# A gated mix of a long convolution and a token MLP: transform tables loaded as constants, and all instructions in a fixed order

## The chip, the cores and the metric

The kernel runs on one core of a Trainium2 chip. The metric is device microseconds (us) of one execution, from the launch's first to last work on the device. The kernel before was run three times: 179.86, 182.16 and 179.96 us, median 179.96. Five engines work side by side and are kept in step by semaphores: TensorE (PE, matrix products), VectorE (DVE), ScalarE (ACT), GpSimd (POOL) and SyncE (SP), which here only issues DMAs.

## The reference

Two branches are mixed by a gate per row. S is 2048, D is 640 and F is 1536; everything is bf16.

```python
g = sigmoid((q * gate_w).sum(-1))
# branch A: short shift convolution of k, times v, then a long convolution
k_shift = sum(k_pad[:, t:t + S, :] * shift_k[:, 3 - t] for t in range(4))
kv = k_shift * v
y = irfft(rfft(kv, 2 * S) * rfft(ssm_k, 2 * S))[:S] + kv * ssm_D
a = q * y
# branch B: an MLP over the tokens
h = layernorm(q)
b = (gelu(h^T @ w1 + b1) @ w2 + b2)^T
out = g * a + (1 - g) * b
```

## The kernel before, in words

**Transforms.** The long convolution is done by a transform of length 4096 at odd frequencies, split into four residues p = 0..3 of the position, and two halves h of the sequence. Inside a residue the transform is a matrix product with tables of cosines and sines, 128 x 128 blocks held in `FTB` (L580, 1 MB over 128 partitions). `fwd` (L880) and `fwd_even` (L896) do it on PE: 320-column matmuls into one of four PSUM slots, evacuated by ACT. The filter `ssm` is transposed on PE first (`transp`, L862, "wtr"), evacuated to `wT`, and transformed ("W"); kv is transformed in two halves ("A"). Between the residues DVE adds and subtracts (`mixing`, `cross`, `product`, `invmix`). `inverse` (L1263) goes back by PE with the same tables in another layout.

**Tables.** They are made on the chip. POOL writes index rows (`brow`, `acol`, eight `jrow`, L806), DVE multiplies and adds them and masks to 12 bits (`prod`, `tb`, `pint`), ACT takes the sine (`sins`, L833). For the inverse, four DMA transposes copy `FTB` to `GTB` (L1044), and later four ACT copies (`gil`, L1114) write them back to `FTB` interleaved.

**MLP.** q is loaded as four blocks `X` of 512 rows. DVE takes the statistics (`bn_stats`, 32 halves, and 16 aggregates), POOL the power -1/2, DVE normalises in place. The first product ("m1") has 12 groups `ft` of 32 matmuls, each group in one PSUM slot, in four parts `hk` of eight; W1 comes in three chunks of four 512 KB pieces through two buffers `ring`. The second product ("m2") has 16 groups of 24 matmuls.

**Short convolution.** k is loaded (`k_load`), permuted by a DVE copy into `kp`, and turned by a DMA transpose to `KT` (`k_turn`, L760); PE multiplies it with banded tap matrices `KF` that POOL built ("kv", 16 short matmuls a group); ACT evacuates and DVE multiplies with v (L1054). `kn` shares the memory of the second ring, so W1's second chunk waits for it.

**Order.** Each engine runs its instructions in the order in which they are emitted. `_Sched.add` (L359) collects operations with their dependencies; `_Sched.run` (L389) simulates them with the estimated durations `dur`, priorities `prio` and PSUM slots while the program is built, and emits in the order found. `chain=True` on a DMA keeps it behind the DMA chained before it. DMAs from SP are issued in order: one that waits holds up those behind it. POOL issues DMAs that add into their target (`accum`). `SPIN` (L798) puts matmuls of zeros ("zz") ahead of the transposes. Lines that many groups share in the profile are those of helpers: L298 is every matmul, L676 every ACT instruction, L632 and L646 DVE or POOL arithmetic, L272 and L265 plain and transposing DMAs.

Of the kernel before, what the change touches and what calls it, by code (L numbers as in the profile page):

```python
# [9 lines left out]
BF16 = mybir.dt.bfloat16  # L10
# [303 lines left out]
class _Op:  # L314
    __slots__ = ("eng", "dur", "emit", "prio", "idx", "ndep", "succ", "vt", "vtrole", "end", "start", "kind", "lat", "deps", "name", "after", "nafter", "asucc", "lock")
# [13 lines left out]
class _Sched:  # L329
# [29 lines left out]
    def add(self, eng, dur, emit, reads, writes, prio=None, vt=None, lat=0.0, name=""):  # L359
# [9 lines left out]
        if vt is not None:  # L369
            vt.left += 1  # L370
            if vt.last_pe is not None:
                deps.add(vt.last_pe)
            if eng == "PE":
                if vt.first is None:
                    vt.first = op
                vt.last_pe = op
            else:
                for d in deps:
                    if d.vt is not vt and not vt.keep:
                        if d not in vt.first.deps:  # L380
                            vt.first.deps.add(d)
        op.deps = deps
        op.after = set()
        self._rec(op, reads, "R")
# [4 lines left out]
    def run(self):  # L389
        ops = self.ops  # L390
        for op in ops:
            op.succ = []
            op.asucc = []
            op.ndep = len(op.deps) + len(op.after)
        for op in ops:
            for d in op.deps:
                d.succ.append(op)
            for d in op.after:
                d.asucc.append(op)
        engs = list(ENGS) + ["SP", "QA"]  # L400
        ready = {e: [] for e in engs}
        pend = {e: [] for e in engs}
        free = {"ACT": 2.93, "DVE": 0.85, "POOL": 0.83, "PE": 1.18, "SP": 0.0, "QA": 0.0}
        port = {"DVE": 0.0, "POOL": 0.0}
        dma_free = 0.3
        avail = {}
        for op in ops:
            avail[op] = 0.0
            if op.ndep == 0:
                heapq.heappush(pend[op.eng], (0.0, op.prio, op.idx))  # L410
        nfree = list(range(self.NSLOT))
        held = {}
        events = []
        order = []
        t = 0.0
        done = 0
        started = 0
        n = len(ops)
        frees = []
        while started < n:  # L420
            while frees and frees[0][0] <= t:
                _, sl, cls = heapq.heappop(frees)
                nfree.append(sl)
                held[cls] -= 1
            nxt = []
            progress = False
            for e in engs:
                while pend[e] and pend[e][0][0] <= t:
                    _, p, i = heapq.heappop(pend[e])
                    heapq.heappush(ready[e], (p, i))  # L430
                if free[e] > t:
                    nxt.append(free[e])
                    continue
                skipped = []
                pick = None
                while ready[e]:
                    p, i = heapq.heappop(ready[e])
                    op = ops[i]
                    if op.vt is not None and op.vt.slot is None:
                        c = op.vt.cls  # L440
                        if not nfree or held.get(c, 0) >= self.limit.get(c, 99):
                            skipped.append((p, i))
                            continue
                    pick = op
                    break
                for s in skipped:
                    heapq.heappush(ready[e], s)
                if pick is None:
                    if pend[e]:
                        nxt.append(pend[e][0][0])  # L450
                    continue
                op = pick
                progress = True
                started += 1
                if op.vt is not None and op.vt.slot is None:
                    op.vt.slot = nfree.pop(0)
                    held[op.vt.cls] = held.get(op.vt.cls, 0) + 1
                op.start = t
                if e in ("SP", "QA") or op.lat < 0:
                    issue = 1.2 if e == "POOL" else 0.1  # L460
                    s = max(t + issue, dma_free)
                    dma_free = s + op.dur
                    op.end = dma_free + 2.0 + (6.0 if e == "POOL" else 0.0)
                    free[e] = t + issue
                else:
                    op.end = t + op.dur
                    if op.lock:
                        op.end += max(port["POOL" if e == "DVE" else "DVE"] - t, 0.0)
                        port[e] = op.end
                    free[e] = op.end  # L470
                order.append(op)
                if op.vt is not None:
                    op.vt.left -= 1
                    if op.vt.left == 0:
                        heapq.heappush(frees, (op.end + 0.05, op.vt.slot, op.vt.cls))
                for s in op.asucc:
                    avail[s] = max(avail[s], op.start)
                    s.ndep -= 1
                    if s.ndep == 0:
                        heapq.heappush(pend[s.eng], (avail[s], s.prio, s.idx))  # L480
                for s in op.succ:
                    lat = 0.08 if s.eng == e else 0.15
                    if e == "PE" and s.eng == "PE":
                        lat = 0.0
                    avail[s] = max(avail[s], op.end + lat)
                    s.ndep -= 1
                    if s.ndep == 0:
                        heapq.heappush(pend[s.eng], (avail[s], s.prio, s.idx))
                nxt.append(free[e])
            if not progress:  # L490
                c = [x for x in nxt if x > t]
                if frees:
                    c.append(frees[0][0])
                assert c, "schedule stuck: " + str([(o.name, o.eng, o.ndep) for o in ops if not hasattr(o, "end")][:12])
                t = min(c)
        self.order = order
        self.makespan = max(o.end for o in ops)
        return order
# [6 lines left out]
def bass_gated_mix__ssm_conv_h3__mixer_token_mlp__prompt_kernel(  # L505
    nc, A_q, A_k, A_v, A_shift_k, A_ssm_k, A_ssm_D, B_x, B_w1, B_b1, B_w2, B_b2, gate_w, out
):
    with nc.Block() as blk:

        @blk.tensor  # L510
        def _(pe_engine):
            _build(nc, A_q, A_k, A_v, A_shift_k, A_ssm_k, A_ssm_D, B_x, B_w1, B_b1, B_w2, B_b2, gate_w, out)


def _build(nc, A_q, A_k, A_v, A_shift_k, A_ssm_k, A_ssm_D, B_x, B_w1, B_b1, B_w2, B_b2, gate_w, out):
# [10 lines left out]
    with ExitStack() as es:  # L526
# [54 lines left out]
        GTB = alloc("GTB", [128, 4, 2, 2, 2, 128], BF16)  # L581
# [6 lines left out]
        acol = alloc("acol", [128, 1], I32, at=base_of(SS))  # L588
        brow = alloc("brow", [128, 128], I32, at=base_of(SS) + 64)
        prod = alloc("prod", [128, 128], I32, at=base_of(SS) + 64 + 2048)  # L590
        tb = alloc("tb", [128, 2, 2, 128], I16, at=base_of(SS) + 64 + 2560)
# [13 lines left out]
        pint = alloc("pint", [128, 4, 2, 2, 256], I16, at=base_of(ring[1]))  # L605
        jrow = alloc("jrow", [128, 8, 256], I16, at=base_of(ring[1]) + 8192)
# [7 lines left out]
        cgb = [alloc(f"cgb{i}", [128, 2, D], BF16, at=base_of(GTB) + 2560 * i) for i in range(3)]  # L614
# [7 lines left out]
        def dve_dur(n, mode):  # L622
            return n / {1: 960.0, 2: 1920.0, 4: 3840.0}[mode] + (0.04 if mode == 4 else 0.08)

        def act_dur(n, nap=0):
            return n / 1200.0 + 0.09 + 0.05 * nap
# [32 lines left out]
        def act(o, i, func, bias=None, scale=None, acc=None, vt=None, prio=None, name="act"):  # L659
# [17 lines left out]
            return SC.add("ACT", act_dur(n_of(o), nap), emit, rr if vt is not None else rr + [i], ww, prio=prio, vt=vt, name=name)  # L677
# [34 lines left out]
        last = [None]  # L712

        def dma(o, i, nbytes, stream="SP", prio=None, sem=None, rate=365.0, chain=False, **kw):
# [7 lines left out]
            if chain:  # L722
                if last[0] is not None:
                    o_.after.add(last[0])
                last[0] = o_
# [14 lines left out]
        def ssm_load(h, a, b):  # L740
            dma(ssm[:, a:b, 1024 * h:1024 * h + 1024], dr(A_ssm_k, 128 * S * a + 1024 * h, [[S, 128], [128 * S, b - a], [1, 1024]]), 128 * (b - a) * 2048, chain=True, rate=({0: 262.0, 1: 223.0}.get(a, RL3)) if h == 0 else 385.0)
# [9 lines left out]
        def x_load(hk):  # L751
            dma(X[:, hk, :, :], dr(A_q, 512 * hk * D, [[4 * D, 128], [1, 4 * D]]), 128 * 5120, chain=True, rate=(352.0 if hk == 0 else 415.0))
# [614 lines left out]
```

## Time and profile before

| what | value |
|---|---|
| median of the three runs | 179.96 us |
| the profiled execution: span from first to last instruction | 178.7 us (the profile gives no other time of it) |
| PE busy | 170.9 us, 1373 matmuls |
| DVE busy | 169.5 us, 203 instructions |
| ACT busy | 117.0 us |
| POOL busy | 43.1 us |
| DMA | 43.51 MB, mean 243 GB/s |
| granted TensorE clock, mean | 0.999 |

PE and DVE columns are the time in which the engine had an instruction in work; the ends of matmuls are modelled and neighbours overlap by some 0.16 us. A line of a timeline has start, length, engine, line of the kernel, operation, written and read names, shape, count, and in brackets the idle time before it with what ended it. A line of the chain of waits has start, length and what the chain ran through. A line of the DMA view has what was loaded, the queue, count, size and the median time from issue to landing.

### The profile page before, as it was taken

The page shows a single profiled execution, that of the slowest core. Times are in us where ns is not written, and L with a number is a line of the kernel's source. Part 1 is how long each engine was busy: PE and PEld are TensorE (multiplying, and loading weights), DVE is VectorE, ACT ScalarE, POOL GpSimd, SP SyncE. Part 2 cuts the span into 40 slices and gives each one's busy share as a digit, 9 for nine tenths or more (in the row PEclk, how much of TensorE's full clock was granted, in tenths as well). Part 3 has the DMA queues.
Part 4 walks back from the last instruction along what each step waited for, and adds up shares of the span by engine and source line. Part 5 has one row for each costly group of instructions (what it writes and reads, how often), then busy time and mean ns, then how long its engine had stood idle before and what let it go on. Part 6 is the DMA issues. An engine that isn't in the chain of part 4 may idle for free.

```text
span 178.7 us, 3326 instructions
## 1 busy us (share of the span) xinstructions
PE 170.9 (96%) x1373; PEld 128.4 (72%) x1374; DVE 169.5 (95%) x203; ACT 117.0 (65%) x176; POOL 43.1 (24%) x52
## 2 busy tenths in 40 slices
PE   7868999899999999999999999999999999999993
PEld 2545787487778677776777778888888887777772
DVE  7799889979999999999999899999999999999984
ACT  4998997999899999428999921131231323753760
POOL 8099803100000065000241100403525000252000
PEclk9999999999999999999999999999999999999999
DMA  5999999999999999999499989797999999599463
GB/s 145 384 413 372 388 301 206 264 421 299 213 258 289 189 272 235 229 229 231 97 244 285 173 132 363 158 229 241 171 194 221 208 201 394 205 164 236 114 233 138
DMA packets 38542, 43.51 MB, mean 243 GB/s; under 512 B 15867, under 2 KB 31360, under 8 KB 38528
## 3 DMA queue, kind: packets, MB, share of 16 engines
q1 hardware_dynamic: 33296, 32.16, 59.1%
q0 software_dynamic: 5200, 11.14, 35.8%
q8 instruction: 11, 0.18, 0.4%
q14 instruction: 3, 0.02, 0.0%
q10 hardware_dynamic: 32, 0.01, 0.0%
HBM read 25.87 MB, written 2.62 MB: 159 GB/s over the span
## 4 chain that ended last, share of the span: by engine, by line
PE 88%; DMA 6%; ACT 3%; SPq 2%; issue 0%; DVE 0%
PE pp L298 88%; DMA rows<-in_B_b_dram 6%; SPq L272 2%; ACT C L676 1%; ACT L676 1%; ACT GT L676 0%; DVE O L688 0%
## 5 line engine op out<-in xcount | busy, mean ns | idle before, releaser
L632 DVE TENSOR_TENSOR C<-C 128x2560 bf16<-128x2560 bf16 (+2 forms) x37 | 54.5, 1525 | 1.1 <-ACT C L676 1.1
L298 PE MATMUL pp<-X,ring 128*128 128x320 bf16 x384 | 55.4, 299 | 0.0
L298 PE MATMUL pp<-GT,W 128*128 128x320 bf16 x384 | 52.6, 299 | 0.0
L298 PEld LDWEIGHTS pp<-GT,W 128*128 128x128 bf16 x384 | 43.6, 114 | 8.6
L298 PEld LDWEIGHTS pp<-X,ring 128*128 128x128 bf16 x384 | 37.3, 98 | 14.3
L676 ACT ACTIVATE C<-pp 128x640 bf16<-128x640 f32 x64 | 40.5, 737 | 3.2 <-PE pp L298 3.2
L676 ACT ACTIVATE O<-pp,c,omg 128x640 bf16<-128x640 f32 x15 | 13.3, 884 | 34.7 <-PE pp L298 34.7
L267 POOL DMA_DIRECT2D C<-C x8 | 11.0, 1615 | 45.0 <-DVE C L632 45.0
L298 PE MATMUL pp<-wT,FTB 128*128 128x320 bf16 x112 | 17.1, 299 | 1.4 <-ACT wT L676 0.8
L676 ACT ACTIVATE cgb<-pp,gg 128x640 bf16<-128x640 f32 x16 | 12.7, 794 | 5.7 <-PE pp L298 5.3
L676 ACT ACTIVATE GT<-pp,cc 128x640 bf16<-128x640 f32 x12 | 9.6, 801 | 9.0 <-PE pp L298 9.0
L298 PEld LDWEIGHTS pp<-wT,FTB 128*128 128x128 bf16 x112 | 10.5, 98 | 6.5 <-ACT wT L676 1.2
L945 DVE BATCH_NORM_STATS2 stats<-X 128x6 f32<-128x320 bf16 x32 | 13.5, 461 | 1.1 <-DMA X<-in_A_q_dram 1.1
L632 DVE TENSOR_TENSOR tm<-C,C 128x2560 bf16<-128x2560 bf16 (+1 forms) x7 | 14.3, 2060 | 0.0
L298 PE MATMUL pp<-C,FTB 128*128 128x320 bf16 x96 | 13.4, 299 | 0.0
L267 POOL DMA_DIRECT2D C<-q_hi x6 | 5.9, 977 | 27.6 <-DVE C L632 13.1
L298 PEld LDWEIGHTS pp<-C,FTB 128*128 128x128 bf16 x96 | 9.3, 98 | 3.8 <-issue 0.2
L676 ACT ACTIVATE gq<-gq 128x640 bf16<-128x640 bf16 x16 | 11.8, 739 | 0.1
L632 DVE TENSOR_TENSOR SS<-C 128x2560 bf16<-128x2560 bf16 x8 | 11.7, 1488 | 0.1
L632 DVE TENSOR_TENSOR C<-tm 128x2560 bf16<-128x2560 bf16 (+1 forms) x9 | 10.7, 1194 | 0.1
L676 ACT ACTIVATE ksh<-pp 128x1024 bf16<-128x1024 f32 (+1 forms) x12 | 9.9, 903 | 0.2 <-PE pp L298 0.2
L676 ACT ACTIVATE wT<-pp 128x1024 bf16<-128x1024 f32 x10 | 9.7, 1027 | 0.6 <-PE pp L298 0.6
(77 smaller groups left out, 188.8 us busy)
## 6 DMA issues: line engine op xcount, KB each, us to landing
ring<-in_B_w_dram SPq DMA_DIRECT2D x12, 512.0 KB, 9.6
W<-in_B_w_dram SPq DMA_DIRECT2D x12, 512.0 KB, 6.3
C<-C POOLq DMA_DIRECT2D x8, 640.0 KB, 10.6
X<-in_A_q_dram SPq DMA_DIRECT2D x4, 640.0 KB, 9.0
kn<-in_A_k_dram SPq DMA_DIRECT2D x4, 640.0 KB, 9.3
out_dram<-O SPq DMA_DIRECT2D x7, 320.0 KB, 3.2
C<-SS POOLq DMA_DIRECT2D x3, 640.0 KB, 11.7
ssm<-in_A_ssm_k_dram SPq DMA_DIRECT2D x3, 512.0 KB, 7.4
```

The source lines that it names most:

```text
L267: ins = engobj.dma_start(out_ap, in_ap, accum_op=ALU.add, max_dma_last_dim=2560)
L272: ins = engobj.dma_start(out_ap, in_ap)
L298: ins = self.nc.tensor.matmul(ps_ap, lhsT=lhsT, rhs=rhs, start=start, stop=stop, skip_group_check=True)
L632: o_ = SC.add(eng, d, lambda s: T.op(eng, lambda e: e.tensor_tensor(o, a, b, op), rd, [o]), rd, [o], prio=prio, name="tt")
L676: return T.op("ACT", lambda e: e.activation(o, src, func, **kw), rr + [src], ww)
L945: ops.append(SC.add("DVE", 0.38, (lambda o, i: lambda s: T.op("DVE", lambda e: e.bn_stats(o, i), [i], [o]))(o, i), [i], [o]))
```

## The change

The tables are computed on the host while the program is built and stored with the program as two constants, `ftab` and `gtab`, 1 MB each. `FTB` is loaded in two DMAs on SP, residues 0 and 2 and then 1 and 3; `GTB`, with a layout of its own for the inverse, in one. All table arithmetic on POOL, DVE and ACT, the four table transposes and the four interleaving copies are removed. The bias rows are loaded from ACT's queue. All matmuls of zeros now stand in one block of 16 at the start. ACT's first instruction is a GELU of one column. Filter blocks 1 and 3 of the first half are evacuated by DVE. `SSM0` is two pieces. The statistics are taken in four groups of four.

The scheduler is removed. `follow` takes a written list of 647 operation numbers, in the sequence of their `add`, as the order, and a string of PSUM slots. Dependencies that only ordered the first matmul of a PSUM slot behind what the evacuation reads become `hint`, which orders nothing.

```diff
+    def follow(self, order, slots):
+        vts, done = {}, set()
+        for op in self.ops:
+            if op.vt is not None and id(op.vt) not in vts:
+                vts[id(op.vt)] = op.vt
+        for vt, s in zip(vts.values(), slots):
+            vt.slot = s
+        self.order = [self.ops[i] for i in order]
...
+def _tables():
+    def cs(k):
+        a = 2.0 * np.pi / 4096.0 * (np.asarray(k, np.int64) % 4096)
+        return np.stack([np.cos(a), np.sin(a)])
...
+                f[:, p, k2, kt] = np.moveaxis(cs(m * (8 * q + 4 * kt + p)), 0, 1)
+            g[:, p, :, k2] = np.moveaxis(cs((4 * (q - 128 * k2) + 1) * (4 * n + p)), 0, 1)
...
+        ftab, gtab = (nc.inline_tensor(a, name=n).ap() for a, n in zip(_tables(), ("ftab", "gtab")))
...
-        SSM0 = ((0, 1), (1, 3), (3, 5))
+        SSM0 = ((0, 2), (2, 5))
+        DVE_EV = (1,3)
+        def tab_load(i, w):
+            dma(V(FTB, 1024 * i, [[2048, 2], [1, w]]), dr(ftab, 2048 * i, [[4096, 128], [1024, 2], [1, w]]), 128 * 4 * w, tok=f"f{i}")
-        small(rows[0:4, 1, :], dr(B_b2, 0, [[512, 4], [1, 512]]), 4096, "SP", chain=True)
+        small(rows[0:4, 1, :], dr(B_b2, 0, [[512, 4], [1, 512]]), 4096, "QA")
...
-        SPIN = (7, 2, 1, 1, 1)
+        SPIN = (0, 0, 0, 0, 0)
+        mms(_VT("cv"), spin(16), name="spin").dur = 5.0
+        act(cst[:, 0:1], cst[:, 1:2], ACT.Gelu_apprx_tanh, name="table").dur = 1.6
-        for p in PORD:
-            t_ = tt("DVE", pv, V(tb, 0, [[0, 2], [256, 2], [1, 256]]), V(jrow, 512 * p, [[256, 2], [0, 2], [1, 256]]), ALU.add)
-            pprev = ts("DVE", pa, pa, 4095, None, ALU.bitwise_and, mode=4)
-            sins[p] = act(FTB[:, p, :, :, :, :].rearrange("q a b c d -> q (a b c d)"), pa, ACT.Sin, bias=cst[:, 0:1],
...
+            if h == 0 and db in DVE_EV:
+                evac_dve(o, i, vt, prio=0)
-            gtbs.append(dma(GTB[:, p, :, :, :, :].rearrange("q a b c d -> q (a b c) d"), FTB[:, p, :, :, :, :].rearrange("q a b c d -> q (a b c) d"), 128 * 2048, rate=200.0, transpose=True, chain=True))
+        dma(GTB[:, :, :, :, :].rearrange("q a b c d -> q (a b c d)"), dr(gtab, 0, [[4096, 128], [1, 4096]]), 128 * 8192, tok="g")
-                    gil = act(V(FTB, 1024 * p, [[1, 2], [256, 4], [2, 128]]), V(GTB, 1024 * p, [[512, 2], [128, 4], [1, 128]]), ACT.Copy, prio=10 ** 5, name="gil")
-        SC.run()
+        SC.follow([int(i) for i in _ORDER.split()], [int(i) for i in _SLOTS])
+_ORDER = """
+8 0 9 4 10 6 11 5 1 13 12 20 16 7 14 21 15 221 26 2 17 27 32 25 29 33 28 22 3 23 18 19 24 36 30 37 34 31 154 40 35 38
...
```

Counted out, the list gives SP this order: filter 512 and 768 KB, X 0, table residues 0 and 2, X 2, table residues 1 and 3, X 1, the filter's second half (768 and 512 KB), X 3, W1 pieces 0 and 1, k 1, W1 2, k 0, gate weights, W1 3, transposes of k 1 and k 0, k 2, k 3, v 0, transpose of k 2, v 1, W1 piece 1 of chunk 1, transpose of k 3, W1 0 of chunk 1, v 3, and then the rest of W1, v 2 and `gtab`.

## The prediction, before the changed kernel was run

> **What bounds the kernel now.** I read the page first, then the chain of work that ended last, then the timelines of TensorE (PE), VectorE (DVE), ScalarE (ACT) and SyncE's queue (SP), then the landings of the loads.
>
> ```profile
> span 178.7 us, 3326 instructions
> PE 170.9 (96%) x1373; PEld 128.4 (72%) x1374; DVE 169.5 (95%) x203; ACT 117.0 (65%) x176; POOL 43.1 (24%) x52
> ```
>
> PE and DVE are both full, so a gain needs both to end earlier. The chain of work says from when PE alone decides:
>
> ```profile
> 4.64 10.14 DMA rows<-in_B_b_dram
> ...
> 14.82 16.34 PE pp L298 x143
> ...
> 32.50 1.28 ACT L676
> ...
> 35.92 140.11 PE pp L298 x1128
> ```
>
> From 35.92 us PE runs 140.11 us without a gap. Whatever is won or lost before that moves the end; behind it only a new wait matters. PE's timeline shows the losses:
>
> ```profile
> 11.41 0.30 PE L298 MATMUL pp<-wT,FTB 128*128 128x320 bf16 x1
> 12.47 1.67 PE L298 MATMUL pp<-wT,FTB 128*128 128x320 bf16 x11 [0.77 <-ACT wT L676]
> 14.82 0.38 PE L298 MATMUL pp<-ident,rows 4*128 4x4 bf16 x5 [0.68 <-DMA rows<-in_B_b_dram]
> 15.13 7.24 PE L298 MATMUL pp<-wT,FTB 128*128 128x320 bf16 x52
> ...
> 34.64 1.04 PE L298 MATMUL pp<-wT,FTB 128*128 128x320 bf16 x4 [0.51 <-ACT GT L676]
> ```
>
> The first transform (wT,FTB) starts at 11.41. It waits for the evacuation of the transposed filter (ACT wT), not for a table. DVE's timeline, start and length in the first two columns, gives a price for dependent neighbours:
>
> ```profile
> 8.28 1.28 DVE L945 BATCH_NORM_STATS2 stats<-X 128x6 f32<-128x320 bf16 x3 [1.08 <-DMA X<-in_A_q_dram]
> ...
> 116.17 1.49 DVE L632 TENSOR_TENSOR C<-C,SS 128x2560 bf16<-128x2560 bf16 x1
> 117.70 1.49 DVE L632 TENSOR_TENSOR C<-tm 128x2560 bf16<-128x2560 bf16 x1
> ```
>
> The second overwrites what the first reads and starts 1.53 us later; independent ones run at 1.40 (two in 2.89).
>
> **The yardstick.** The page gives the execution's span, 178.7 us, and no other time of its own. The runs' median is 179.96, so 1.26 us lie around the span; I carry them over.
>
> PE between 11.41 and 35.92 (24.51 us): 136 matmuls of 320 columns (64 first transform, 56 MLP, 16 second transform) at 0.136 us (320 of them in 43.63) are 18.5; 40 transposes (24 in 1.65, 16 in 1.15) 2.5; constants 0.3. That is 21.3 of work and 3.2 of loss. So PE's end = start of the first transform + 21.3 + 140.1 + waits; before, 11.4 + 21.3 + 3.2 + 140.1 = 176.0.
>
> **The change, part by part.**
>
> *Table arithmetic out.* Gone are eight DVE operations on pint (4 x 0.68 + 4 x 0.43 = 4.4 us), three on prod and tb (0.9), ten POOL iotas, and four Sin (3.36 + 1.14 = 4.5 on ACT). None ends a wait of PE after 4.3 us; three Sin do delay the first evacuation to 7.02. The last filter piece ended PE's wait at 9.63 and two evacuations (2.04) followed. Alone their removal is worth nothing, covered by the filter's load; without that cover the 1.9 us from 5.15, when the first transposes ended, to 7.02.
>
> *Tables in by DMA, another order of loads.* Landings before, from issue plus time to landing, by megabytes queued: 0.79 at 6.3 us, 1.44 at 8.3, 1.97 at 9.6, 2.6 at 11.2, 3.9 at 14.1, 5.8 at 19.5: 2.5 to 2.8 us per MB. The order list, counted out, loads filter (1.31 MB), X block 0, half the table, X 2, the other half, X 1, second filter half, X 3, W1. Hence filter 7.8, X 0 9.6, first tables 10.8, second 13.7, W1's first piece 22.2 (before 19.5). The last transposes run 7.9 to 10.0; two of five evacuations move to DVE; the last on ACT ends at 11.1. First transform at 11.2: -0.2. No row shows a 1024-column evacuation on DVE. Nearest are ACT's, 0.92 each (five in 4.69), and the final DVE reads of PSUM, 0.55 for 320 columns, so 1.76 if scaled. I take 1.15, nearer to ACT's row; the upper end puts DVE 0.6 later, the lower 0.2 earlier. DVE sits idle there until X 0.
>
> *Spins.* Sixteen 512-column matmuls stand at the front. The first seven took 3.16, so 0.43 each; a later pair 0.59, so 0.215 each. Half and half they end at 6.4, all at 0.43 at 8.1; the filter's second piece at 7.8 covers the first and leaves 0.3 of the other.
>
> *The early constants and the table load.* Bias rows go to ACT's queue before X, so PE's stop from 14.1 to 15.13 (1.0) goes. One activation table at the start replaces the load at 32.50, and PE's 0.51 behind it goes. The row has the next ACTIVATE 1.30 us after that load began. [...]
>
> *What is late next at the start.* Thirteen evacuations at 0.60 (14 in 8.45) from 11.9 end at 19.7. Two wide (0.92) and two narrow ones then free the PSUM slot of the first MLP group: 22.8. Its W1 (22.2) and its normalised X (22.5, after X 3's first statistics at 21.1) come just before. PE's own work ends at 11.2 + 10.6 = 21.8: a wait of 1.0.
>
> *Table transposes and interleaving copies out.* Four DMA transposes held SP for 9.97 us (51.7 to 61.7) and four ACT copies took 5.1. W1's third chunk waits behind the former but is used from about 90; ACT sat idle 9.0 us for PE around the latter. Worth nothing under that cover (up to 10 us if the chunk were wanted at 62); one 1 MB load on SP replaces them, used after 150.
>
> *The fixed order.* SP is where it can bite:
>
> ```profile
> 24.03 7.36 SPq L265 DMA_TRANSPOSE KT<-kp  x2
> 31.43 1.06 SPq L272 DMA_DIRECT2D vkv<-in_A_v_dram  x2
> ```
>
> A transpose of k holds SP 3.7 us. Before, all four v loads went out ahead of the second pair; now v 1 is queued behind transpose 2, which waits for a DVE copy, which waits for k 2. From statistics at 9.8: 30 halves (0.383), 14 aggregates (0.09) and 10 applies (0.36) are 16.4, with 0.5 for X 3's landing: copy of k 1 at 26.7, of k 0 ending at 29.9. Transposes hold SP 27.4 to 34.8. k 2 lands 4.9 later, like the first load behind transposes before (vkv): 39.7. DVE reaches its copy at 38.4 and waits 1.3. Transpose 2 holds SP 40.5 to 44.2; v 1 is issued then. For its landing the loads' rows (median us last) give the ends:
>
> ```profile
> vkv<-in_A_v_dram SPq DMA_DIRECT2D x2, 640.0 KB, 5.4
> v<-in_A_v_dram SPq DMA_DIRECT2D x2, 640.0 KB, 9.5
> ```
>
> Singly 4.9 to 10.5. I take 4.9, as it too is the first plain load behind a transpose: 49.1. DVE wants it at 40.5 + 5 x 1.405 + 0.735 = 48.2, waits 0.9 and multiplies until 50.5. PE's order needs the product 26.5 us after the first MLP group (14 MLP groups of 1.087, 17 transform groups, 80 short matmuls in 4.2): 49.3. With PE's list fixed, nothing fills: a wait of 1.4. The other gates have covers of 0.3 to 3 us, for which I put 0.2: last normalised X 34.2 against 35.3, k transposed 37.8 against 40.7. On POOL the tap products (8.14) run from 7.6 and the scales follow from 15.8, wanted at 18.6. Late on POOL three accumulating DMAs move behind that of the third product, to 133 (first before 124.5); at 10.6 us they land by 146.4, wanted at 147.5.
>
> *DVE.* Busy 163.3 us between 8.28 and 176.6, idle 5.0. Now it starts at 9.8 and idles 3.5 (0.5, 1.3, 0.9, and 0.8 in small gaps). Of some twenty dependent neighbours about ten are pulled apart, 0.13 each, -1.3. End 9.8 + 163.3 - 1.3 + 3.5 = 175.3, 1.3 earlier, level with PE. [...]
>
> **Sum.** PE ends at 11.2 + 21.3 + 140.1 + 1.0 + 1.4 + 0.2 - 0.3 (constants now earlier) = 174.9, 1.1 before the old 176.0. The end behind it is unchanged. 179.96 - 1.1 = 178.8 us.
>
> **The rivals.**
>
> *v 1 comes late (slower).* At 10.5 us it lands at 54.7; PE waits 54.7 + 1.6 - 49.3 = 7.0 instead of 1.4: 184.4. It is slower than before from a landing time of about 6 us, slower by over 2% from 9.7. For it: DMA busy at 1.0 or more there. Against: little is queued ahead of it.
>
> *DVE is the bound.* If pulling pairs apart saves nothing, DVE ends at 176.6: 180.0. For it: 95% busy. Against: the 1.53.
>
> *The tables' megabyte delays all that follows.* 2.7 us on X, W1 and k instead of the 1.0 counted: 180.5. For it: DMA full until 45 us. Against: X 0 is early.
>
> *No wait at all (faster).* Start 0.5 earlier, no waits: 178.8 - 2.6 - 0.5 = 175.7. For it: every gate is within 2 us. Against: four would have to hold.
>
> *The change does nothing.* The tables were never waited for, and PE and DVE stay full: 180.0.
>
> **How the numbers follow.** Likeliest 0.45 (own range 177.2 to 180); DVE bound, late tables or no change 0.32 (179.5 to 181.5); v 1 late 0.14, most of it over 2%; no wait 0.09. 2%, about what a measurement of this kernel tells from no change, is 176.4 to 183.6. Faster 0.09, same 0.79, slower 0.12. The range runs from 176.0 to 183.6 and leaves out the ends of the last two cases.
>
> **What would show it.** First transform at 11.2; first MLP matmul at 22.8; no second table load; PE's only long gap near 49, ended by DVE's product, with DVE waiting for v 1 shortly before; last matmul near 175. It is wrong if the first transform starts after 12, if v 1 lands over 6 us after its issue, if dependent neighbours are as common as before on DVE, or if PE stops after 60 us.

## The result, and the profile after

The changed kernel took 186.53 us (median of four runs, 185.21 to 187.26), the kernel before 179.91 (four runs, 179.31 to 182.16) beside it: a ratio of 1.035, 95% interval 1.029 to 1.042. The prediction was 178.8 us, with a range that ended at 183.6. Ratios leave out single runs more than 1.5% above the fastest of their kernel; medians do not.

The profiled execution took 185.21 us with a span of 183.1, so 2.1 us lie around the span. Before, the span was 178.7. Of the 6.6 us between the medians the profiles hold 4.4. Another 1.3 is that the profiled run is the fastest of the four. The other 0.9 comes from the profiled run of before, which was not typical: seventeen later runs of that kernel with spans of 177.8 to 178.2 took 179.6 to 180.1 us, 1.8 to 2.0 us around the span, not the 1.26 that the prediction worked out of a span and another run's median.

The first lines of the page after:

```profile
span 183.1 us, 3314 instructions
PE 173.2 (95%) x1377; PEld 128.8 (70%) x1377; DVE 166.8 (91%) x193; ACT 105.0 (57%) x166; POOL 42.0 (23%) x45
```

ACT lost 12 us of work and DVE 2.7, as the removed arithmetic and the two evacuations that moved from ACT to DVE should give. The time is longer all the same, so it went into waits or behind the last work. The chain of waits (start, length, what it ran through) names the first of them:

```profile
23.96 21.54 PE pp L298 x192
...
55.83 11.29 DMA ring<-in_B_w_dram
...
67.17 8.06 PE pp L298 x58
```

PE's 140 us without a gap are gone: a load of a W1 piece, issued at 55.83, ends in a wait of PE. PE's timeline shows its size, and the start:

```profile
1.18 5.67 PE L298 MATMUL pp<-zz 128*128 128x512 bf16 x16 [1.18 <-DVE zz L614]
...
11.43 0.30 PE L298 MATMUL pp<-wT,FTB 128*128 128x320 bf16 x1 [0.23 <-ACT wT L593]
12.31 7.10 PE L298 MATMUL pp<-wT,FTB 128*128 128x320 bf16 x51 [0.58 <-ACT wT L593]
...
67.17 2.35 PE L298 MATMUL pp<-X,ring 128*128 128x320 bf16 x16 [1.91 <-DMA ring<-in_B_w_dram]
```

Behind 75 us the chain leaves PE. It runs through ACT, then through DVE and POOL's accumulating DMAs, and comes back only for the last 56 matmuls:

```profile
136.24 14.89 DMA C<-C
...
168.79 1.50 DVE SS L549
...
170.34 7.79 PE pp L298 x56
```

The second half of the loss is at the end. SyncE's queue, before and after:

```profile
142.79 1.61 SPq L272 DMA_DIRECT2D q_hi<-in_A_q_dram  x2
145.74 5.12 SPq L272 DMA_DIRECT2D q_lo<-in_A_q_dram  x2
158.94 18.04 SPq L272 DMA_DIRECT2D out_dram<-O  x9
```

```profile
148.06 0.34 SPq L272 DMA_DIRECT2D q_lo<-in_A_q_dram  x1
148.45 1.24 SPq L272 DMA_DIRECT2D q_hi<-in_A_q_dram  x1
156.37 0.33 SPq L272 DMA_DIRECT2D q_lo<-in_A_q_dram  x1
156.75 0.43 SPq L272 DMA_DIRECT2D q_hi<-in_A_q_dram  x1
170.46 9.14 SPq L272 DMA_DIRECT2D out_dram<-O  x9
```

Before, both `q_hi` blocks were issued from 142.79 on, ahead of `q_lo`, and the nine output writes were spread over 158.94 to 176.98. Now the second `q_hi` is queued behind a `q_lo` load that waits until 156.37 for an accumulating DMA of POOL, and the nine outputs all go out in the last 13 us. DVE's last operation ends at 178.7, and the span goes on for 4.4 us instead of 2.1. The loss of span is thus 2.1 us of PE (last matmul at 178.13 against 176.03) and 2.3 behind DVE.

### The profile page after: what moved, and what is told of

It is laid out like the page before. It is cut to its first block, busy times and chain, and to the rows that moved or that the text cites. A ratio compares the mean times of both kernels' runs of the same rounds, so it can differ in the third digit from the quotient of the medians.

```text
span 183.1 us, 3314 instructions
## 1 busy us (share of the span) xinstructions
PE 173.2 (95%) x1377; PEld 128.8 (70%) x1377; DVE 166.8 (91%) x193; ACT 105.0 (57%) x166; POOL 42.0 (23%) x45
## 4 chain that ended last, share of the span: by engine, by line
DVE 32%; PE 31%; DMA 20%; ACT 10%; issue 3%; POOL 1%; SPq 0%; DVEq 0%
PE pp L298 31%; DVE C L549 17%; DMA C<-C 8%; ACT C L593 7%; DMA ring<-in_B_w_dram 6%; DVE tm L549 6%; DMA C<-q_hi 5%; DVE q_hi L549 4%; DVE SS L549 3%; ACT wT L593 2%; ACT gq L593 1%; DVE gq L549 1%; POOL C L267 1%; SPq L272 0%; DVE O L605 0%
## 5 line engine op out<-in xcount | busy, mean ns | idle before, releaser
L298 PE MATMUL pp<-X,ring 128*128 128x320 bf16 x384 | 57.2, 299 | 2.2 <-DMA ring<-in_B_w_dram 1.9
L549 DVE TENSOR_TENSOR C<-C 128x2560 bf16<-128x2560 bf16 (+2 forms) x37 | 55.3, 1524 | 2.2 <-ACT C L593 1.7
L593 ACT ACTIVATE C<-pp 128x640 bf16<-128x640 f32 x64 | 42.7, 727 | 12.5 <-PE pp L298 12.3
L298 PE MATMUL pp<-wT,FTB 128*128 128x320 bf16 x112 | 17.8, 299 | 0.8 <-ACT wT L593 0.8
L593 ACT ACTIVATE cgb<-pp,gg 128x640 bf16<-128x640 f32 x16 | 12.0, 792 | 5.8 <-PE pp L298 5.8
L298 PEld LDWEIGHTS pp<-wT,FTB 128*128 128x128 bf16 x112 | 10.5, 98 | 5.3 <-ACT wT L593 0.8
L298 PE MATMUL pp<-C,GTB 128*128 128x320 bf16 x96 | 13.4, 300 | 0.0
L298 PEld LDWEIGHTS pp<-C,GTB 128*128 128x128 bf16 x96 | 9.1, 98 | 4.1 <-ACT cgb L593 0.4
L267 POOL DMA_DIRECT2D O<-q_hi x4 | 4.8, 1326 | 28.0 <-DVE q_hi L549 28.0
L267 POOL DMA_DIRECT2D C<-q_hi x6 | 5.9, 1121 | 18.3 <-DVE gg L564 10.5
```

The costliest lines, as they stand in the source:

```text
L267: ins = engobj.dma_start(out_ap, in_ap, accum_op=ALU.add, max_dma_last_dim=2560)
L298: ins = self.nc.tensor.matmul(ps_ap, lhsT=lhsT, rhs=rhs, start=start, stop=stop, skip_group_check=True)
L549: o_ = SC.add(eng, d, lambda s: T.op(eng, lambda e: e.tensor_tensor(o, a, b, op), rd, [o]), rd, [o], prio=prio, name="tt")
L593: return T.op("ACT", lambda e: e.activation(o, src, func, **kw), rr + [src], ww)
```

## The experiments

All ratios are to the kernel before, run beside it on the same chip; brackets hold the 95% interval. The diffs of orders give the queue's sequence in words.

### W1's third piece moved up (e_ring)

```diff
  SP: ... transpose k 3, W1 chunk 1 piece 0,
+ W1 chunk 1 piece 2,
  v 3, W1 chunk 2 piece 0, W1 chunk 1 piece 3, W1 chunk 2 piece 2, v 2,
- W1 chunk 1 piece 2,
```

> The changed kernel with one load moved in SP's list: W1 chunk 1 piece 2 directly behind piece 0 instead of behind v 3, three other pieces and v 2. Theory P (PE decides, its 1.9 us wait at 65.3 us is the late landing of this piece at 67.1): the wait goes and the end comes 1.5 to 2 us earlier, about 184.7 against the changed kernel's 186.5 median. Rival D (DVE decides behind it): the wait goes and the end stays within 0.5 us.

184.62 us, 1.022 [1.015, 1.030]: 1.9 us less than the changed kernel by the medians. All four runs (184.31 to 184.82) lie under all four of the changed kernel, though the intervals just touch. PE's wait is gone; the same 24 matmuls run through:

```profile
64.74 3.42 PE L298 MATMUL pp<-X,ring 128*128 128x320 bf16 x24
```

It was the place on the queue, not the load's size, that made the wait. What it was worth is less certain. Between the medians it is the wait's length, theory P. In the two profiled runs the spans differ by 0.5 us (183.1 and 182.6), which is rival D's figure; the zeros at the front took 0.58 longer in this one, so 1.1 us is won between the first MLP matmul and PE's last group. Two pieces of W2 now hold PE for 0.75 us (0.26 for one in the changed kernel).

### Evacuations back on ACT (e_evac)

```diff
-        DVE_EV = (1,3)
+        DVE_EV = ()
```

> The changed kernel with all five filter evacuations of the first half on ACT instead of two on DVE. The first statistics on DVE begin at about 8.5 us instead of 10.6, the first transform at about 12.3 as now. Theory D (DVE's late start is carried to the end): 1.5 to 2 us earlier than the changed kernel's 186.5. Rival P (PE decides): within 0.7 us of it.

185.85 us, 1.030 [1.021, 1.039]. DVE starts its statistics at 8.38 instead of 10.60 but then waits 0.8 and 1.0 us for X. The interval overlaps that of the changed kernel: a gain is not shown, and the 0.7 us between the medians is rival P's figure.

### The end reordered, alone and with q_hi moved up (e_tail, e_q, e_qtail)

```diff
  e_tail, e_qtail:
  PE: inverse h 0,
+ one group of the second product (24 matmuls),
  inverse h 1, ...
  DVE: products of h 0 ahead of the combination for h 1; SP: outputs of h 0 first
  e_q, e_qtail:
  SP: q_lo 1, q_hi 0,
+ q_hi 1,
  q_lo 0,
- q_hi 1,
```

> The changed kernel with the order of its last 25 us changed: the second product's group (3,0) stands behind the first half's inverse instead of before it, DVE finishes the first half's inverse combination and its four products with q before the second half's, and SP writes the first half's four blocks before the second half's. Theory S (the nine output writes all fall into the last 9 us, so 4.4 us pass after the last vector instruction against 2.1 before): the span behind that instruction falls to 2 to 3 us and the time by 1.5 to 2.5, to about 184.5. Rival W (the last write is slow for another reason): no change, within 0.7 us of 186.5.

189.19 us, 1.048 [1.039, 1.056], slower still; both expected figures were missed. The trace shows why. DVE's timeline:

```profile
164.22 0.83 DVE L549 TENSOR_TENSOR q_hi<-cgb,q_hi 128x1280 bf16<-128x1280 bf16 x1 [5.82 <-DMA q_hi<-in_A_q_dram]
```

The load was issued at 157.68. An order that wants the products early cannot have them while `q_hi` stands behind the waiting `q_lo`.

> The changed kernel with one DMA moved: the load of q_hi's second block goes on SP directly behind that of the first, instead of behind q_lo's first block, which waits for an accumulating DMA of POOL. It should be issued near 150 us instead of 156.75 and land near 157 instead of 162.3. Theory Q (the crowded end comes from this load AND from an order on DVE that was written around its late landing): DVE has no idle time before 162.38 in the changed kernel, so the earlier landing alone buys nothing: 186 to 187, end behind the last matmul 4.0 to 5.0 us as before. Rival L (the load alone crowds the end): the four products of the first half come earlier, outputs start before 168, the end behind the last matmul falls to 2.0 to 3.0 us, 183.5 to 185.0.

185.11 us, 1.030 [1.026, 1.035]. Not resolved: 0.5% under the changed kernel's ratio, with overlapping intervals, and between the two expected ranges. The span still ends 4.6 us behind DVE's last operation (178.4) and 5.2 behind the last matmul. So theory Q holds in its main point: the load moved alone does not clear the end.

> As the run before, and with the other order at the end that was slower when run alone (189.2 us): one group of the second product behind the first half's inverse, the first half's products on DVE ahead of the second half's combination, its outputs first on SP. Alone it made DVE wait 5.82 us for the load that is now moved up. Theory Q: that wait goes and PE's two waits of 2.58 and 2.03 us behind it; the last matmul comes at 177.5 to 179.5, the end behind it is 2.0 to 3.0 us, 182.0 to 185.0 in all. Rival B (the nine outputs need their time wherever they stand, 9.1 us from first to last): the end stays at 4 to 5 us behind the last matmul and the time at 185.5 or more.

186.56 us, 1.039 [1.033, 1.045]. Both expected figures were missed. The 5.82 us are down to 1.6, and the span's end is 2.1 us behind DVE's last operation, so the outputs no longer crowd. But PE waits 2.29 us between the two halves of the inverse, and the 32 matmuls behind that took 6.51 us, where the same 32 take 4.83 in the next run:

```profile
167.21 6.51 PE L298 MATMUL pp<-C,GTB 128*128 128x320 bf16 x32 [2.29 <-DVE C L549]
```

### The edits together (e_rqt)

> As the run before, and W1's piece moved as in the run that took away PE's wait at 65 us (-1.9 us alone). Theory Q with P: the two gains add, 180.0 to 183.0, PE without a wait over 0.6 us behind 24 us. Rival B: 183.5 to 185.0, since only the first gain shows.

184.04 us, 1.022 [1.014, 1.029], but two runs at 182.48 and 183.12 and two at 184.95 and 185.62. The profile is of the best one. SP's queue and PE's end in it:

```profile
145.53 0.34 SPq L272 DMA_DIRECT2D q_lo<-in_A_q_dram  x1
145.92 2.89 SPq L272 DMA_DIRECT2D q_hi<-in_A_q_dram  x2
...
162.00 16.83 SPq L272 DMA_DIRECT2D out_dram<-O  x9
```

```profile
165.42 4.83 PE L298 MATMUL pp<-C,GTB 128*128 128x320 bf16 x32 [2.20 <-DVE C L549]
```

The outputs start 8.5 us earlier than in the changed kernel, and the span ends 2.15 us behind DVE's last operation (178.45), as before the change. So the crowded end is repaired by both edits together, and 180.6 us of span is 2.5 under the changed kernel. Of this 0.7 is luck: the zeros took 4.96 us here, the shortest of all profiles, for 5.67. In time the repair of the end is not shown: against e_ring, which has only W1's piece moved, the median is 0.6 us less and the ratio the same. The better two runs had a mean granted clock of 1.000, the other two 0.991, so the spread goes with the clock in these four.

### The gap filled (e_rqt2, e_rqt3)

```diff
  PE: inverse h 0, a group of the second product (24 matmuls),
+ 16 matmuls of another group, which stood before the inverse,
  inverse h 1
```

> The three edits of the fixed order (W1's piece, q_hi's block, the end reordered) with TensorE's gap of 2.2 us between the two halves of the inverse filled: 16 matmuls of the second product are moved behind the 24 that already stand there, 40 as in the kernel before. With the gap, runs of the three edits lay at spans of 180.6 and 181.1 at a granted clock of 1.00 and at 183.0 and 183.6 at 0.991; three other profiles with a gap of 2.0 to 2.7 us there show a granted clock of 0.68 to 0.77 in the microseconds behind it. Theory C (the gap lets the clock fall, and that is the spread): mean clock 0.995 or more in every run, spread under 1.5 us, 181.0 to 182.6. Rival (the gap and the spread have nothing to do with each other): runs on both sides of 183.5 again.

183.31 us, 1.014 [1.006, 1.022], all four runs at a clock of 1.000 and within 1.1 us. Theory C holds for clock and spread in these four runs. That the gap alone makes the clock fall does not follow: e_best, below, has a gap of 2.38 us at the same place and keeps its clock. The time is 0.7 us over the expected range, because the gap reopened ahead: 0.98 us for an evacuation and 1.30 us for DVE's combination.

```profile
147.35 3.45 PE L298 MATMUL pp<-GT,W 128*128 128x320 bf16 x24 [0.98 <-ACT O L593]
152.09 8.92 PE L298 MATMUL pp<-C,GTB 128*128 128x320 bf16 x64 [1.30 <-DVE C L549]
```

This is the best fixed order measured, still slower than the kernel before.

> As the run before, and all evacuations of the transposed filter on ACT (0.7 us less than the changed kernel when done alone); sixteen matmuls of zeros in one block. If the gain adds: 180.3 to 182.0. Not under the kernel before, since DVE's work behind 8.4 us is that of the kernel before: an end under 179.4 would refute that.

184.80 us, 1.022 [1.013, 1.031]: the expected gain is not there. Runs lie at 183.5 and 183.7 (clock 1.00) and twice at 185.9 (clock 0.99), this time, in the profiled one, for a slow stretch at the front, shown below.

### The tables' load taken away (e_notab)

```diff
-            dma(V(FTB, 1024 * i, ...), dr(ftab, 2048 * i, ...), 128 * 4 * w, tok=f"f{i}")
+            memset("DVE", V(FTB, 1024 * i, [[2048, 2], [1, w]]), 0.01)
```

> The changed kernel without the load of the 1 MB transform table at the front: DVE fills it with one number instead (two memsets in its idle time before 7.7 us), so the values are wrong and all else is in place. Leaves 1 MB, some 2.6 us of loads, out of the way of X, W1 and k. Theory G (the front is set by the filter's transposes, their evacuations and ACT's chain up to the first MLP group, not by loads): first transform at 11.2 to 11.6, first MLP matmul at 23.5 to 24.2, time within 1.0 us of the changed kernel's 186.5. Rival M (the tables' megabyte delays all that follows): first statistics still at 10.6 but the later blocks earlier, first MLP matmul at 21.5 to 22.8, 183.5 to 185.0.

185.89 us, 1.035 [1.030, 1.040], the ratio of the changed kernel to the third digit. First transform at 11.97, first MLP matmul at 24.50, both 0.54 later than in the changed kernel, since the zeros took 6.21 us in this execution and 5.67 there. In this order the megabyte's absence saves nothing that an interval of half a percent shows: theory G.

### Parts of the change without its order (e_b4load, e_b4best, e_b4rows, e_list)

```diff
  e_b4load, in the kernel before:
-            sins[p] = act(FTB[:, p, ...], pa, ACT.Sin, ...)
+        tab_load(0)
         x_load(1)
+        tab_load(1)
  e_b4best, besides:
-        small(rows[0:4, 1, :], ..., "SP", chain=True)
+        small(rows[0:4, 1, :], ..., "QA")
+        act(cst[:, 0:1], cst[:, 1:2], ACT.Gelu_apprx_tanh, prio=-1, name="table").dur = 1.6
  e_b4rows, in the kernel before: only the bias rows to ACT's queue
```

> The kernel before, with one part of the change alone: the forward tables are loaded as a constant (1 MB in two DMAs on SP, behind X 0 and X 1), and the index rows, DVE's table arithmetic and the four Sin are left out. Everything else, the scheduler, the transposes of the table for the inverse and the interleaving copies, stays as before. Theory O (the tables were never waited for and cost nothing either way; the loss of the whole change is in its new order): 178.5 to 181.0, within 1% of the kernel before, first transform at 10.9 to 12.0. Rival T (the megabyte of tables at the front delays X, W1 and k, and that is the loss): 182.5 to 186.0.

181.73 us, 1.011 [1.007, 1.015]: between the two theories' figures. PE now waits 0.56 us for W1 and 0.96 for the bias rows, and DVE 1.3 for X 1 and 1.5 for k.

> The kernel before with all parts of the change except its order: forward tables loaded and not computed, bias rows from ACT's queue, the GELU's table loaded at the start; the scheduler and the transposes of the table for the inverse stay. With the tables alone it took 181.7 us, PE stopped 0.96 us for the bias rows, 0.56 for W1 and 0.51 behind the second table load, DVE 1.3 for X 1 and 1.5 for k. Theory O (the order loses most of the 6.6 us, the tables by their place ahead of X 1 to k some 1 to 2): 180.3 to 181.5. Rival N (without those stops the parts gain as the prediction had it): 178.0 to 179.5.

181.01 us, 1.006 [1.003, 1.009]. Theory O. PE's only wait of over half a microsecond behind the first transform is for W1, which is now queued behind the tables:

```profile
22.70 1.26 PE L298 MATMUL pp<-X,ring 128*128 128x320 bf16 x8 [1.56 <-DMA ring<-in_B_w_dram]
```

So the tables, the bias rows and the GELU's table together cost 1.1 us where the scheduler sets the order. It finds that order anew in each of these builds, so the rest does not stay fixed. The other 5.5 us of the changed kernel (186.5 against 181.0) belong to the fixed order with what it fixes, the new load list, the zeros, the evacuations on DVE and `gtab` in place of the table transposes.

> The kernel before, with one small part of the change alone: the two bias rows are loaded from ACT's queue instead of SP's, behind X. It takes away PE's stop at 14.1 to 15.13 us. Theory G (DVE is full and sets the end together with PE, so 1.0 us on PE alone is worth half of it or less): 179.2 to 179.9. Rival W (PE alone decides behind 35.9 us, as the prediction had it): 178.6 to 179.1.

180.05 us, 1.001 [0.998, 1.005]. PE loses the stop but the time does not change. This does not show that a gain at the front is lost behind it. In the profile the first transform starts at 12.20 instead of 11.41, since PE's waits for the filter ended later:

```profile
12.20 0.30 PE L298 MATMUL pp<-wT,FTB 128*128 128x320 bf16 x1
12.90 8.98 PE L298 MATMUL pp<-wT,FTB 128*128 128x320 bf16 x63 [0.41 <-ACT wT L676]
21.85 1.25 PE L298 MATMUL pp<-X,ring 128*128 128x320 bf16 x8
```

So the first MLP matmul came only 0.36 us earlier (21.85 for 22.21), and PE's last group came 0.36 earlier too (172.24 for 172.60).

The run e_list kept the other parts of the change but handed the order back to the scheduler, with the new load list as a chain and with the PSUM slots' old dependencies:

```diff
-                        vt.first.hint.add(d)
+                        vt.first.deps.add(d)
...
-        SC.follow([int(i) for i in _ORDER.split()], [int(i) for i in _SLOTS])
+        for a, b in zip(ORDER, ORDER[1:]):
+            toks[b].after.add(toks[a])
+        SC.run()
```

> The changed kernel with its loaded tables, its loads and its evacuations, but the order found again by the list scheduler of the kernel before (loads chained in a plain sequence, dependencies of a PSUM slot's first matmul as before). Theory O (the written order costs the time, the tables do not): 178 to 181.5 us, with the wait for a W1 piece near 65 us and the crowded end gone. Rival T (the 1 MB of tables in front of the loads, or the constants themselves, cost the time): 184 us or more.

188.19 us, 1.042 [1.035, 1.050]. The figure of T was met. Its reason does not show in the trace: PE waits at 30.97 and 35.93 for DVE's normalised X (1.33 and 1.02 us) and at 40.97 for POOL's tap products (1.05), which the scheduler had put behind the scales. It tells that the new load list and the old scheduler do not fit, and nothing of the tables alone.

### The zeros at the front (e_spin8, e_zint, e_best, e_best2)

```diff
  e_spin8:
-        mms(_VT("cv"), spin(16), name="spin").dur = 5.0
+        mms(_VT("cv"), spin(8), name="spin").dur = 5.0
  e_zint:
+        mms(_VT("cv"), spin(7), name="spin").dur = 5.0
...
+            if h == 0:
+                items = spin({0: 2, 3: 1, 2: 1, 4: 1}.get(db, 0)) + items
  e_best = e_rqt + e_evac + e_spin8; e_best2 = e_rqt + e_evac + e_zint
```

> The changed kernel with 8 instead of 16 matmuls of zeros at the front. In the profiles so far the sixteen took 4.96 to 6.25 us and the first transform started 4.6 us behind their end each time, at 10.7 to 12.0. Theory Z (the zeros hold up the filter's transposes, whose load has long landed): first transform at 9.8 to 10.6, first MLP matmul about 1 us earlier, time 184.5 to 186.0. Rival F (the filter's second piece or the table's landing at 10.2 takes the zeros' place at once): first transform at 11.2 to 11.8, 186.0 to 187.2.

186.43 us, 1.033 [1.025, 1.040], runs from 184.5 to 188.7. In the profiled one, which was the fastest, the first transform starts at 10.28, as theory Z had it, and waits for the table, as rival F had it: with the zeros out of the way the megabyte does become a gate.

```profile
4.59 0.72 PE L298 MATMUL pp<-ident,ssm 128*128 128x128 bf16 x8
...
10.28 7.26 PE L298 MATMUL pp<-wT,FTB 128*128 128x320 bf16 x52 [0.96 <-DMA FTB<-ftab]
```

> All edits that gained, together: W1's piece moved, q_hi's second block moved up, the end reordered, 8 matmuls of zeros, and all evacuations of the transposed filter on ACT, so that DVE starts its statistics when X 0 lands. If the gains add (184.0 for the first three, 1.0 for the zeros, 0.7 for the evacuations): 180.5 to 183.0. If DVE, with some 167 us of work, is the bound by then, the last two give only what DVE starts earlier (about 2 us, less what it then waits for X 1): 181.5 to 183.5. If it is under 179.4 the fixed order can beat the kernel before.

185.07 us, 1.026 [1.020, 1.033], profiled at a span of 184.0. The gains did not add. With the same 8 zeros PE ran slowly here:

```profile
4.92 1.07 PE L298 MATMUL pp<-ident,ssm 128*128 128x128 bf16 x8
...
12.34 9.42 PE L298 MATMUL pp<-wT,FTB 128*128 128x320 bf16 x51 [0.85 <-ACT wT L593]
```

Eight transposes take 1.07 us instead of 0.72, and 51 matmuls 9.42 instead of some 7.1. The next expectation reads this as a rate of 0.18 us up to 21.6 us. It is a mean of two rates: nine of these matmuls were in work between 14 and 16 us, seventeen between 18 and 20. What eight zeros saved at the front in e_spin8, a slow PE took back here: the first 52 matmuls of the transform end at 21.76 us for 17.54 there. At the end this run has a gap of 2.38 us, and its clock stays at 1.00:

```profile
168.88 4.84 PE L298 MATMUL pp<-C,GTB 128*128 128x320 bf16 x32 [2.38 <-DVE C L549]
```

> The changed kernel with its sixteen matmuls of zeros spread as in the kernel before: 7 at the front, 2, 1, 1, 1 ahead of the second to fifth transposed block and 1 ahead of the first transform, 13 in all. With 8 at the front and none between, one profile ran at the full rate from 4.4 us (128-column transposes 0.71 us for eight), another at about two thirds of it until 21.6 us (1.07 for eight, 320-column matmuls 0.18 instead of 0.136 us). Theory K (PE must be kept in matmuls to keep its rate, and the block of 16 buys that by delaying the filter by 1 to 2 us): rate full from 5 us on, first transform at 10.2 to 11.0, 184.5 to 185.8, spread of the runs under 1.5 us. Rival (the spread has another cause): some runs over 187.

186.22 us, 1.034 [1.028, 1.039], runs from 184.6 to 186.6. Theory K's figures were missed: in the profiled run PE was slow until about 10.5 us (eight transposes took 1.07 us up to 9.7, 0.80 from 10.26 and 0.71 from 11.72) and the first transform started at 12.49, as late as the latest with the block of sixteen (10.73 to 12.49).

> The edits of the fixed order together, with the zeros spread as in the run before: W1's piece and q_hi's block moved up, the end reordered, all evacuations of the transposed filter on ACT. Theory D (DVE's 163 us of work behind 8.4 us is the same as in the kernel before, and so is what it waits): 180.0 to 182.0, not under the kernel before. Rival: the front's gain shows at the end, under 179.0.

184.70 us, 1.026 [1.020, 1.033]. Slower than expected by both. PE's front was quick in the profile (first transform 10.95), but PE then waited for the product of v 1, the gate that the prediction had computed, and the clock fell behind the gap at the end:

```profile
51.52 0.99 PE L298 MATMUL pp<-vkv,FTB 128*128 128x320 bf16 x6 [1.44 <-DVE vkv L549]
```

Three windows of the end, with PE's busy time first and the granted clock third from the end:

```profile
160.00:164.00 4.00, 4.00 (x31) 3.25 (x30) 4.00 (x5) 2.23 (x4) 2.13 (x3) 1.00 0.68 106
164.00:167.00 3.00, 0.46 (x4) 0.12 (x2) 3.00 (x4) 0.88 (x1) 2.06 (x2) 1.00 1.07 224
167.00:171.00 4.00, 3.74 (x18) 2.15 (x19) 3.96 (x4) 0.07 (x1) 0.16 (x1) 0.68 1.13 217
```

PE stands for 2.66 us, and in the window behind that it is granted 0.68. In the profiled runs of e_rqt and e_best gaps of 2.20 and 2.38 us at the same place left the clock at 1.00.

## Why the prediction was wrong, step by step

Two steps failed: the term of 0.2 us for "the other gates" on PE, which left out the late W1 piece (1.91 us), and the end behind PE, put at no change (2.3 us longer). Added up for the profiled run: 178.8, plus 3.2 for PE's last matmul (178.13 for 174.9), plus 2.3 for the end behind it, plus 0.85 around the span (2.11 for 1.26), is 185.2. PE's 3.2 are 1.1 from the front, 0.7 from waits (2.3 for 1.6) and 1.4 from short gaps.

**First transform at 11.2: the time held (11.43) by luck, the reason did not.** The prediction let the filter's landing at 7.8 gate the transposes and hid sixteen zeros behind it. The filter is there by 6.84 us (the load that e_spin8 waits for), and the transposes began at 6.94, when the zeros ended. In eleven profiles with sixteen zeros these took 4.96 to 6.37 us, and the start moves with them.

**X 0 at 9.6 and DVE from 9.8.** X 0 lands by 8.4 (e_evac). DVE was held until 10.60 by the two evacuations that the change gave it, at 1.23 us each for the estimated 1.15. "DVE sits idle there until X 0" was the failing step.

```profile
9.46 1.23 DVE L599 CAST wT<-pp 128x1024 bf16<-128x1024 f32 x1 [0.55 <-PE pp L298]
10.60 1.66 DVE L849 BATCH_NORM_STATS2 stats<-X 128x6 f32<-128x320 bf16 x4
```

**The front: 1.1 us later than predicted.** The work that ended at 35.92 before ends at 34.3 now (136 matmuls of 320 columns counted in the timeline). It was to end at 33.2. So the front gained 1.6 us.

**v 1: right.** Issued at 44.09 (44.2) and landed at 49.0 (49.1); DVE multiplied from 49.11. PE came there at 50.69, too late to wait, so the predicted 1.4 us did not appear. Part of the match is luck: the copy for the transpose began 0.6 us late (40.27 for 39.7), and the transpose held SP for 2.92 us instead of 3.7. The gate itself is real: e_qtail and e_best2 wait there for 0.64 and 1.44 us. The rival of a late v 1 fell.

**"The other gates ... for which I put 0.2": failed.** PE waited 1.91 us for W1 chunk 1 piece 2, and 0.42 in two other places. The prediction followed v 1 down SP's queue and stopped there; the pieces behind it, issued after a transpose that held SP 4.94 us and in an order that puts W1 chunk 2 ahead of chunk 1, were not followed to their use. The prediction had named a stop of PE after 60 us as a sign of being wrong. In e_ring the wait is gone, and 1.1 us (profiles) to 1.9 us (medians) with it. Besides, PE lost some 1.4 us in gaps too short for a line of their own. Two stretches make 0.9 of it: the 160 matmuls of the taps went at 0.054 instead of 0.051 us, the 96 of the inverse's first groups at 0.140 instead of 0.136. The rest was not told apart.

**DVE: end 178.7, not 175.3.** Start +0.8, idle 5.2 for 3.5, and work 162.9 us for 162.0. The saving of 1.3 from dependent neighbours pulled apart came to 0.4. The row was right (1.53 us still from 125.55 to 127.08, 1.40 from 119.69 to 121.09), the count was not.

**"The end behind it is unchanged": failed, 2.3 us.** Only PE's and DVE's ends were predicted. That a `q_hi` load stood behind a waiting `q_lo` could be read from the order list. DVE's order, which puts the first half's products late, was not followed to the outputs either. e_q and e_tail show that neither edit alone repairs it, e_rqt that both do (2.15 us).

**Second table load: gone (the one that is left starts at 2.32 us), its worth not measured alone.** e_b4best, which removes it and the stop for the bias rows, takes 0.7 us less than e_b4load, with intervals that overlap, and is not under the kernel before. The premise "whatever is won or lost before that moves the end" is too strong for gains. In e_b4best the first 136 matmuls of 320 columns end at 34.46 instead of 35.92 and PE's last matmul ends at 175.0 instead of 176.03, but DVE's last operation ends at 176.9, 0.3 later than before. In e_b4rows the small gain of 0.36 us did reach the end.

**The rivals.** "The tables' megabyte delays all that follows" is refuted for this order (e_notab) and half right for the old one (e_b4load, +1.1%). "The change does nothing" held for the tables in the fixed order alone. "DVE is the bound" was nearly right on the saving (0.4 us for its 0) and missed the end. "No wait at all" fell. "v 1 comes late" was of the right kind, a load kept back by the written queue, but at the wrong place: W1's piece and `q_hi` were the late ones.

What stays open: the last 2.6 us between the best fixed order (e_rqt2) and the kernel before are seen as several waits of 0.2 to 1.5 us on both engines, and were not told apart.

## What to carry to other kernels

The scheduler of the kernel before finds the order anew whenever an operation or a load changes; a written order stays as it is. So follow every DMA on a queue, past the first one of interest, to the instruction that uses it, and ask of each waiting DMA what is queued behind it. Predict the end of the kernel by its outputs, not by its last arithmetic. Work that was hidden (here the tables' arithmetic) brought no gain when a load replaced it (e_b4load, 1.011), and the load still had to be given a place on a queue.

## What the runs showed of the hardware

**TensorE's rate at the front differed between executions that begin with the same matmuls.** Matmuls of 512 columns ran at 0.43 us and later at 0.215 (in the kernel before seven in 3.16 us and then two in 0.59, each stretch with an overlap of 0.16), and the change came at different times: the first five took 2.31 or 2.32 us in all eleven profiles with sixteen, all sixteen 4.96 to 6.37. In e_best the slow rate lasted until between 16 and 18 us: 40 transposes went at 1.07 us for eight (0.71 in the changed kernel), the first matmul of 320 columns took 0.45 us (0.30 there), and nine of them were in work from 14 to 16 us against seventeen from 18 to 20, while the granted clock in the records read 1.00. What sets the time of the change is not shown.

**Gaps of under three microseconds were followed by a lower clock in some profiles.** Gaps of 2.29, 2.58 and 2.66 us (e_qtail, e_tail, e_best2) were followed by a granted clock of 0.59 to 0.77 over windows of 3 to 4 us; gaps of 2.03, 2.20 and 2.38 us (e_tail, e_rqt, e_best) were not. With one profile of each, this gives no threshold. At the front of e_rqt3 the clock fell behind two stops of only 0.58 and 0.53 us:

```profile
12.00:14.00 2.00, 0.98 (x5) 0.59 (x6) 2.00 (x7) 1.35 (x3) 2.00 (x2) 0.90 1.03 420
14.00:16.00 2.00, 2.00 (x9) 1.09 (x8) 2.00 (x7) 1.41 (x2) 2.00 (x2) 0.50 1.05 395
16.00:18.00 2.00, 2.00 (x13) 1.30 (x12) 1.74 (x6) 1.46 (x3) 2.00 (x2) 0.75 1.06 403
```

In e_evac the same two stops (0.59 and 0.53 us) left the clock at 1.00, and its 51 matmuls took 7.10 us instead of 8.78:

```profile
12.54 7.10 PE L298 MATMUL pp<-wT,FTB 128*128 128x320 bf16 x51 [0.53 <-ACT wT L593]
```

So the length of the stop does not decide alone, and what else does was not tested. A wait of PE cost well over its length in e_best2: the 2.66 us, and 1.6 more until the clock was back (the same 32 matmuls took 6.47 us there and 4.83 in e_rqt).

**Constants stored with the program showed no cost outside the span.** With 2 MB of them the time around the span was 1.75 to 2.23 us, without them (the kernel before and e_b4rows) 1.75 to 2.25.
